# Sharing projection weights between two chunks and staging weight sums in another buffer, in a fused attention and feed-forward kernel

## The chip, the cores and the metric

The kernel runs on one core of one Trainium2 chip. The metric is the device time of one execution in microseconds (us), given as the median of the runs. The kernel before took 834.39 us (median of 3 runs, 833.3 to 835.75).

The engines are named as in the profile: PE (TensorE, matmuls), PEld (its weight loads), DVE (VectorE), ACT (ScalarE), POOL (GpSimd) and SP (SyncE). SP and POOL also issue DMA transfers. In these traces each engine runs its own instructions in a fixed order and stops at the first one that has to wait: in one run below, DVE stood 19.9 us at one operation with others behind it.

## The reference

```python
# x: 2048 x 1024 bf16; 32 heads of 32; window W = 8, dilation 2; feed-forward width 3584
def reference(A_x, A_wqkv, A_wo, B_x, B_w_gate, B_w_up, B_w_down, gate_w):
    x = A_x
    g = sigmoid((x * gate_w).sum(-1, keepdims=True))
    q, k, v = split_heads(x @ A_wqkv)
    # ... each row attends to rows s, s-2, ..., s-14 (those that exist), softmax
    a = o @ A_wo
    h = gelu(x @ B_w_gate) * (x @ B_w_up)
    b = h @ B_w_down
    return g * a + (1 - g) * b
```

## The kernel before

The 2048 rows are cut into four chunks of 512. The feed-forward part works on two chunks at once (a "super") with a seven-product scheme for 2x2 blocks. For that scheme it needs sums and differences ("forms") of x and of the weights. The forms of the down and wo weights are computed once, early, by `prep_down`. That routine loads weight rows, subtracts them on DVE, and stores the forms in DRAM. The parts that the change touches are these; cuts are marked with "...".

```python
ring = ctx.enter_context(tc.tile_pool(name="ring", bufs=5))   # five 1 MB weight tiles
hT = persist.tile([P, 2 * NST, FT, P], BF16)                  # the FFN's hidden values

def qkv_load(which, pieces):          # two ring tiles for q, k or v weights, loaded by SP
    ...
def qkv(c):
    ...
    for which in range(3):
        tiles = qkv_load(which, ...)  # each chunk loads q, k and v weights anew
        ...                           # 64 matmuls, evictions on ACT (and DVE for q of chunk 0)

def x_forms():                        # four DVE operations; the FFN of a super needs all of them
    b11, b21, b12, b22 = xr[:, 0], xr[:, 1], xr[:, 2], xr[:, 3]
    with hp():
        nc.vector.tensor_tensor(out=tf[:, 0], in0=b12, in1=b11, op=ALU.subtract)
        nc.vector.tensor_tensor(out=tf[:, 1], in0=b22, in1=tf[:, 0], op=ALU.subtract)
        nc.vector.tensor_tensor(out=tf[:, 2], in0=b21, in1=tf[:, 1], op=ALU.subtract)
        nc.vector.tensor_tensor(out=b12, in0=b22, in1=b12, op=ALU.subtract)   # "the last x form"

def load_xT(c):                       # eight DMA transposes of x into xr
    for kt in range(KT):
        nc.sync.dma_start_transpose(out=xT(c, kt), in_=x[s0:s0 + SC, kt * P:(kt + 1) * P])

def prep_down(i0, n):                 # called nine times: seven for w_down, two for wo
    ...
        st = ring_tile()              # loaded rows
        ...                           # two loads of 512 KB, issued by POOL
        ot = ring_tile()              # the sums
        fo = ...
        nc.vector.tensor_tensor(out=fo[:, 0], in0=b12, in1=b11, op=ALU.subtract)
        nc.vector.tensor_tensor(out=fo[:, 1], in0=b22, in1=fo[:, 0], op=ALU.subtract)
        nc.vector.tensor_tensor(out=fo[:, 2], in0=b22, in1=b12, op=ALU.subtract)
        nc.vector.tensor_tensor(out=fo[:, 3], in0=b21, in1=fo[:, 1], op=ALU.subtract)
        ...                           # four stores of 256 KB to DRAM, issued by POOL

qkv(0)
...
load_xT(1)
gate(0)
for i0 in range(0, NPREP, 2):
    prep_down(i0, min(2, NPREP - i0))
    if i0 == 6:
        attention(0)                  # DVE work almost alone
qkv(1)
gate(1)
attention(1)
for sup in range(NSUP):
    x_forms()
    ffn(sup)
    ...
```

The program order is not the order on an engine: a scheduler interleaves independent work, and `hp()` raises the priority of what it encloses. `q`, `k` and `v` below are the three parts of the qkv projection.

## Time and profile before

| Reading | Before | View |
|---|---|---|
| median of runs | 834.39 us | times |
| span of the profiled run, granted clock | 833.0 us, 0.950 | page, list of cores |
| PE / DVE busy | 90% / 73% | page, part 1 |
| longest idle stretch of PE | 53.17 us from 56.5 us | timeline of PE |
| SP's longest wait for a ring tile | 71.4 us | waits of SP |
| last x form starts | 158.17 us | timeline of DVE |
| last product of the first FFN ends | 340.09 us | timeline of DVE |

First come lines of the page of the kernel before. Part 1 has busy time, share and instruction count per engine. In part 2 each digit is the busy share, in tenths, of one fortieth of the span (20.8 us); PEclk is the granted clock.

```profile
span 833.0 us, 9110 instructions
PE 746.3 (90%) x3345; PEld 370.1 (44%) x3413; DVE 608.4 (73%) x908; ACT 307.6 (37%) x513; POOL 54.1 (6%) x99
...
PE   7970069899999999799999989979999999999998
...
DVE  1688997999899999771197998998999943641201
...
PEclk8995569999999999899999999989999999999999
DMA  9568884535465465999736895325444444689985
```

The row of PE has two zeros at slices 4 and 5 and nothing like them later. The clock falls to 5 in the same place. DVE and DMA are busy there.

The timeline of PE before has start, length, engine, line, operation, output and inputs, count, and in brackets the idle time before it with what ended it.

```profile
10.73 44.09 PE L137 MATMUL ps<-xr,rg 128*128 128x512 bf16 x188 [3.96 <-DVE xr L518]
54.66 1.89 PE L171 MATMUL pz<-xr,gwb 128*128 128x512 bf16 x8
109.72 3.21 PE L137 MATMUL ps<-xr,rg 128*128 128x512 bf16 x7 [53.17 <-DMA rg<-in_A_wqkv_dram]
```

After the gate of chunk 0 nothing runs for 53.17 us, until a load of qkv weights for chunk 1 lands. The first seven matmuls after the hole take 3.21 us, twice their usual time.

The waits of SP's queue before give total, count and longest in us.

```profile
SPq L129 <- DMA dforms<-rg: 71.4, 1, 71.4
```

This is why the weights were late: the load had to wait for a ring tile that the staging still held until its stores to DRAM ended.

The table of stretches before has start and end, length, busy time (count) of PE, PEld, DVE, ACT and POOL, then granted clock, DMA share and GB/s.

```profile
55.00:110.00 55.00, 1.83 (x9) 0.69 (x7) 48.51 (x110) 3.48 (x5) 23.60 (x41) 0.55 0.84 294
155.00:325.00 170.00, 163.90 (x735) 73.69 (x749) 163.94 (x248) 101.35 (x171) 6.93 (x13) 0.99 0.49 160
```

In the hole DVE is busy 48.5 of 55 us, so DVE limits how much of it can be won. In the FFN, PE and DVE are both full: 163.9 of 170 us.

The FFN can't run on without the last x form. The timeline of DVE before shows when it comes:

```profile
158.17 1.22 DVE L252 TENSOR_TENSOR xr<-xr 128x2048 bf16<-128x2048 bf16 x1
```

### The profile page before, as it was taken

Reading aid. Unit: us, or ns where it says so; the run is one execution under the profiler, and the core shown is the slowest. Engines: PE = TensorE matmul, PEld = TensorE weight load, DVE = VectorE, ACT = ScalarE, POOL = GpSimd, SP = SyncE. Lnnn points to the kernel's source line nnn. Section 1 sums busy time; section 2 is a strip of 40 time slices with the busy share of each in tenths; the row PEclk is TensorE's granted clock in tenths of the full one; section 3 lists DMA queues with packets and bytes.
Section 4 is the critical chain, followed back from the end, with each engine's and each line's share of the span. In section 5 each row is a group of like instructions: output and inputs, shape, how many; then the busy total and the mean of one; then the engine's idle time right before and its main releaser. Section 6 shows DMA issues by size and latency. Waiting matters only on the chain.

```text
span 833.0 us, 9110 instructions
## 1 busy us (share of the span) xinstructions
PE 746.3 (90%) x3345; PEld 370.1 (44%) x3413; DVE 608.4 (73%) x908; ACT 307.6 (37%) x513; POOL 54.1 (6%) x99
## 2 busy tenths in 40 slices
PE   7970069899999999799999989979999999999998
PEld 4640036444444444344664446634444444444443
DVE  1688997999899999771197998998999943641201
ACT  1321014555755457110333104347557555310110
POOL 0044400000000000001000010000000000001000
PEclk8995569999999999899999999989999999999999
DMA  9568884535465465999736895325444444689985
GB/s 307 147 231 296 257 326 134 169 101 159 146 202 157 149 200 164 256 312 331 262 116 220 312 344 171 114 67 173 141 134 168 146 143 160 223 289 312 327 310 185
DMA packets 124491, 174.13 MB, mean 209 GB/s; under 512 B 17696, under 2 KB 96544, under 8 KB 120864
## 3 DMA queue, kind: packets, MB, share of 16 engines
q1 hardware_dynamic: 115488, 136.33, 50.5%
q0 software_dynamic: 8672, 36.71, 12.1%
q8 instruction: 26, 0.43, 0.2%
q10 hardware_dynamic: 288, 0.52, 0.2%
q14 instruction: 17, 0.14, 0.1%
HBM read 142.08 MB, written 28.31 MB: 205 GB/s over the span
## 4 chain that ended last, share of the span: by engine, by line
issue 47%; PE 26%; DVE 17%; DMA 5%; POOL 3%; ACT 2%; POOLq 0%; DVEq 0%; ACTq 0%
PE pB L324 5%; PE qB L447 5%; PE qD L447 4%; PE qA L447 4%; DMA rg<-in_B_w_down_dram 3%; PE pD L324 3%; PE pA L324 3%; DVE prod L202 3%; DVE acc L203 2%; PE ps L137 2%; DVE pall L240 2%; POOL fforms L306 1%; DMA gcol<-in_gate_w_dram 1%; DVE accT L205 1%; DVE hT L350 1%
## 5 line engine op out<-in xcount | busy, mean ns | idle before, releaser
L324 PEld LDWEIGHTS <-rg 128*128 128x128 bf16 x1568 | 154.2, 98 | 203.6 <-issue 22.1
L137 PE MATMUL ps<-xr,rg 128*128 128x512 bf16 x752 | 172.1, 389 | 60.9 <-DMA rg<-in_A_wqkv_dram 56.0
L137 PEld LDWEIGHTS <-rg 128*128 128x128 bf16 x768 | 110.5, 144 | 122.0 <-DMA rg<-in_A_wqkv_dram 58.5
L324 PE MATMUL pB<-tf,rg 128*128 128x512 bf16 x439 | 114.7, 381 | 4.2 <-DVE hT L363 3.6
L324 PE MATMUL pA<-xr,rg 128*128 128x512 bf16 x439 | 114.1, 380 | 2.9 <-ACT pB L344 2.1
L447 PEld LDWEIGHTS <-hT 128*128 128x128 bf16 x672 | 66.3, 99 | 86.2 <-issue 4.7
L447 PE MATMUL qB<-rg,hT 128*128 128x512 bf16 x330 | 76.3, 379 | 0.5 <-DMA rg<-dforms 0.2
L203 DVE TENSOR_TENSOR acc<-acc,prod 128x2048 bf16<-128x2048 bf16 x56 | 68.3, 1220 | 1.2
L324 PE MATMUL pB<-xr,rg 128*128 128x512 bf16 x218 | 57.5, 382 | 5.2 <-DVE og L181 4.7
L324 PE MATMUL pD<-xr,rg 128*128 128x512 bf16 x220 | 56.9, 379 | 2.4 <-ACT m_1678 L358 1.3
L324 PE MATMUL pD<-tf,rg 128*128 128x512 bf16 x220 | 58.7, 388 | 0.2
L447 PE MATMUL qA<-rg,hT 128*128 128x512 bf16 x220 | 54.0, 394 | 4.5 <-DMA rg<-in_B_w_down_dram 4.2
L350 DVE TENSOR_TENSOR hT<-hT,gl 128x1024 bf16<-128x1024 bf16 x56 | 38.3, 685 | 15.5 <-ACT hT L349 15.2
L344 ACT COPY pB<-pA 128x512 f32<-128x512 f32 x56 | 32.2, 576 | 32.8 <-PE pA L324 31.8
L369 ACT ACTIVATE gl<-pA 128x512 bf16<-128x512 f32 x56 | 33.6, 599 | 27.4 <-PE pA L324 25.2
L451 POOL DMA_DIRECT2D out_dram<-ost x24 | 13.0, 541 | 446.9 <-ACT ost L473 339.7
L491 DVE SCALAR_TENSOR_TENSOR ost<-qB,omg,m5d 128x512 bf16<-128x512 f32 x8 | 6.0, 748 | 47.1 <-issue 28.7
L240 DVE TENSOR_TENSOR pall<-ab,vT_85 128x2048 bf16<-128x2048 bf16 x32 | 38.9, 1217 | 0.0
L240 DVE TENSOR_TENSOR pall<-ab,vT_86 128x2048 bf16<-128x2048 bf16 x32 | 38.9, 1216 | 0.0
L505 ACT ACTIVATE ost<-qB,omg 128x512 bf16<-128x512 f32 x8 | 5.5, 687 | 87.6 <-PE qB L447 87.6
L202 DVE TENSOR_TENSOR prod<-qo_81,kT_83 128x2048 bf16<-128x2048 bf16 x28 | 34.2, 1222 | 1.9 <-ACT kT_83 L164 0.5
L349 ACT CAST hT<-pB 128x512 bf16<-128x512 f32 x56 | 32.2, 575 | 7.5 <-PE pB L324 7.5
(649 smaller groups left out, 846.5 us busy)
## 6 DMA issues: line engine op xcount, KB each, us to landing
rg<-dforms SPq DMA_DIRECT2D x32, 896.0 KB, 7.0
rg<-in_A_wqkv_dram SPq DMA_DIRECT2D x22, 1024.0 KB, 8.3
rg<-in_B_w_down_dram SPq DMA_DIRECT2D x24, 896.0 KB, 6.3
rg<-in_B_w_gate_dram SPq DMA_DIRECT2D x28, 512.0 KB, 4.0
fforms<-rg POOLq DMA_DIRECT2D x14, 1024.0 KB, 6.1
rg<-fforms SPq DMA_DIRECT2D x14, 1024.0 KB, 4.8
rg<-oforms SPq DMA_DIRECT2D x16, 512.0 KB, 3.7
rg<-in_B_w_down_dram POOLq DMA_DIRECT2D x14, 512.0 KB, 4.9
```

The lines of the kernel that those rows point to most:

```text
L137: nc.tensor.matmul(ps[:], lhsT=lhsT, rhs=xT(c, kt), start=(kt == 0), stop=(kt == KT - 1))
L202: nc.vector.tensor_tensor(out=prod[:], in0=q_b, in1=k_w, op=ALU.mult)
L203: nc.vector.tensor_tensor(out=acc[:], in0=acc[:], in1=prod[:], op=ALU.add)
L205: nc.vector.transpose(out=accT[:].rearrange("p c d -> p (c d)"), in_=acc[:].rearrange("p w s -> p (w s)"))
L240: nc.vector.tensor_tensor(out=pall[:], in0=ab[:], in1=v_w, op=ALU.mult)
L324: nc.tensor.matmul(bk[:], lhsT=w, rhs=rhs[:, k, :], start=(start and k == 0), stop=(k == KH - 1), skip_group_check=True)
L344: nc.scalar.copy(out=Bk[f][:], in_=A[f][:])
L349: nc.scalar.copy(out=hs(f, 0), in_=v3(Bk[f][:]))
L350: nc.vector.tensor_tensor(out=hT[:, :, f, :], in0=hT[:, :, f, :], in1=gl[f][:].rearrange("p (j s) -> p j s", s=P), op=ALU.mult)
L369: nc.scalar.activation(out=gl[f][:, 0:SC], in_=A[f][:], func=ACT.Gelu_apprx_tanh)
L447: nc.tensor.matmul(bk[:], lhsT=l, rhs=w[i], start=(start and i == 0), stop=(i == n - 1), skip_group_check=True)
L451: eng.dma_start(out=o2[s0 + j * P:s0 + (j + 1) * P, nh * NW:(nh + 1) * NW], in_=ost)
```

## The change

Its intent is to remove the hole. The q, k and v weights are loaded once and kept for both chunks 0 and 1 (6 MB less to load; v weights lie in part of `hT`, which is idle then). The staging of the weight sums moves out of the ring into five stages in `hT`. The gate gets a higher priority. The transposes of chunk 1 move ahead of the q weights in SP's queue, and `attention(0)` moves from after the fourth of the nine stagings to after the last.

```diff
-    def qkv_load(which, pieces):
+    def qkv_load(which, pieces, vbuf=False):
         tiles = []
         for hf in range(2):
-            wt = ring_tile()
-            wv = wt[:].rearrange("p (k n) -> p k n", k=KH)
+            if vbuf:
+                wv = hT[:, hf * KH:(hf + 1) * KH, 0:NT, :].rearrange("p k f n -> p k (f n)")
+            else:
+                wv = ring_tile()[:].rearrange("p (k n) -> p k n", k=KH)
 ...
+    def stage():
+        f0 = 8 + 4 * (stage_n[0] % 5)
+        stage_n[0] += 1
+        return hT[:, :, f0:f0 + 4, :].rearrange("p (a b) f s -> p a b (f s)", b=2)
 ...                                    # in prep_down:
-            st = ring_tile()
+            st = stage()
+            sa, sb = st[:, 0:m, :], st[:, 2:2 + m, :]
+            for dst, r in ((sa, b), (sb, nr + b)):
+ ...
+                for k in range(m):     # four loads of 256 KB a staging, instead of two of 512 KB
+                    nc.gpsimd.dma_start(out=dst[:, k], in_=v[:, k])
-            ot = ring_tile()
+            fo = stage()[:, :, 0:m, :]
 ...
-    qkv(0)
+    load_xT(1)
+    wq = qkv_load(0, [(k, k + 1) for k in range(KH)])
+    qkv_outer(0, 0, wq)
+    wk = qkv_load(1, [(0, KH)])
+    qkv_one(0, 1, wk)
 ...
-    load_xT(1)
-    gate(0)
+    wv = qkv_load(2, [(0, KH)], vbuf=True)
+    qkv_one(0, 2, wv)
+    with hp():
+        gate(0)
     for i0 in range(0, NPREP, 2):
         prep_down(i0, min(2, NPREP - i0))
-        if i0 == 6:
-            attention(0)
-    qkv(1)
-    gate(1)
+    attention(0)
+    halo(1)
+    qkv_one(1, 0, wq)
+    qkv_one(1, 1, wk)
+    qkv_one(1, 2, wv)
+    with hp():
+        gate(1)
     attention(1)
 ...                                    # the other two gates get hp() too
```

More of the change, by code (lines that the diff above doesn't have):

```diff
@@ L137, in qkv_mm, with halo @@
         nc.tensor.matmul(ps[:], lhsT=lhsT, rhs=xT(c, kt), start=(kt == 0), stop=(kt == KT - 1))
-    def qkv(c):
+    def halo(c):
         cc = c % 2
@@ L144, in qkv, with qkv_dst, qkv_outer, qkv_one @@
             nc.scalar.copy(out=vT[cc][:, :, 0:HALO], in_=vT[pc][:, :, SC:SC + HALO])
-        for which in range(3):
-            tiles = qkv_load(which, [(k, k + 1) for k in range(KH)] if (c == 0 and which == 0) else [(0, KH)])
-            dsts = [(qo[cc][:, t, :], kT[cc][:, t, HALO:HALO + SC], vT[cc][:, t, HALO:HALO + SC])[which]
-                    for t in range(NT)]
-            if c == 0 and which == 0:
-                banks = [bank("ps") for t in range(NT)]
-                for kt in range(KT):
-                    for t in range(NT):
-                        qkv_mm(banks[t], tiles, t, kt, c)
-                for t in range(NT):
-                    if t % 2 == 0:
-                        nc.scalar.copy(out=dsts[t], in_=banks[t][:])
-                    else:
-                        nc.vector.tensor_copy(out=dsts[t], in_=banks[t][:])
-            else:
-                for t in range(NT):
-                    ps = bank("ps")
-                    for kt in range(KT):
-                        qkv_mm(ps, tiles, t, kt, c)
-                    nc.scalar.copy(out=dsts[t], in_=ps[:])
+    def qkv_dst(c, which, t):
+        cc = c % 2
+        return (qo[cc][:, t, :], kT[cc][:, t, HALO:HALO + SC], vT[cc][:, t, HALO:HALO + SC])[which]
+    def qkv_outer(c, which, tiles):
+        banks = [bank("ps") for t in range(NT)]
+        for kt in range(KT):
+            for t in range(NT):
+                qkv_mm(banks[t], tiles, t, kt, c)
+        for t in range(NT):
+            if t % 2 == 0:
+                nc.scalar.copy(out=qkv_dst(c, which, t), in_=banks[t][:])
+            else:
+                nc.vector.tensor_copy(out=qkv_dst(c, which, t), in_=banks[t][:])
+    def qkv_one(c, which, tiles):
+        for t in range(NT):
+            ps = bank("ps")
+            for kt in range(KT):
+                qkv_mm(ps, tiles, t, kt, c)
+            nc.scalar.copy(out=qkv_dst(c, which, t), in_=ps[:])
+    def qkv(c):
+        halo(c)
+        for which in range(3):
+            qkv_one(c, which, qkv_load(which, [(0, KH)]))
     gates = {}
@@ L257, in load_xT @@
             nc.sync.dma_start_transpose(out=xT(c, kt), in_=x[s0:s0 + SC, kt * P:(kt + 1) * P])
+    stage_n = [0]
+    def stage():
+        f0 = 8 + 4 * (stage_n[0] % 5)
+        stage_n[0] += 1
+        return hT[:, :, f0:f0 + 4, :].rearrange("p (a b) f s -> p a b (f s)", b=2)
     def prep_down(i0, n):
@@ L264, in prep_down @@
             b, m = (lo[0] if kind == "d" else lo[0] - FH), len(lo)
-            st = ring_tile()
-            sa = st[:, 0:2 * D].rearrange("p (k n) -> p k n", k=2)[:, 0:m, :]
-            sb = st[:, 2 * D:4 * D].rearrange("p (k n) -> p k n", k=2)[:, 0:m, :]
-            if kind == "d":
-                nc.gpsimd.dma_start(out=sa, in_=src[b * P:(b + m) * P, :].rearrange("(k p) n -> p k n", p=P))
-                nc.gpsimd.dma_start(out=sb, in_=src[(FH + b) * P:(FH + b + m) * P, :].rearrange("(k p) n -> p k n", p=P))
-            else:
-                nc.gpsimd.dma_start(out=sa, in_=AP(src.tensor, src.offset + b * D, [[NT * D, P], [D, m], [1, D]]))
-                nc.gpsimd.dma_start(out=sb, in_=AP(src.tensor, src.offset + (NTH + b) * D,
-                                                   [[NT * D, P], [D, m], [1, D]]))
-            ot = ring_tile()
-            fo = ot[:].rearrange("p (f k n) -> p f k n", f=4, k=2)[:, :, 0:m, :]
-            b11, b12, b21, b22 = sa[:, :, 0:NW], sa[:, :, NW:D], sb[:, :, 0:NW], sb[:, :, NW:D]
+            st = stage()
+            sa, sb = st[:, 0:m, :], st[:, 2:2 + m, :]
+            for dst, r in ((sa, b), (sb, nr + b)):
+                if kind == "d":
+                    v = src[r * P:(r + m) * P, :].rearrange("(k p) (h n) -> p k h n", p=P, h=2)
+                else:
+                    v = AP(src.tensor, src.offset + r * D, [[NT * D, P], [D, m], [NW, 2], [1, NW]])
+                for k in range(m):
+                    nc.gpsimd.dma_start(out=dst[:, k], in_=v[:, k])
+            fo = stage()[:, :, 0:m, :]
+            b11, b12, b21, b22 = sa[:, :, 0], sa[:, :, 1], sb[:, :, 0], sb[:, :, 1]
             nc.vector.tensor_tensor(out=fo[:, 0], in0=b12, in1=b11, op=ALU.subtract)
@@ L545 @@
             qkv(c0 + 2)
-            gate(c0 + 2)
+            with hp():
+                gate(c0 + 2)
             attention(c0 + 2)
@@ L551 @@
             qkv(c0 + 3)
-            gate(c0 + 3)
+            with hp():
+                gate(c0 + 3)
             attention(c0 + 3)
```

## The prediction

> **What bounds it now.** The page gives 833.0 us, PE busy 90%. The PE timeline has one large hole: the gate of chunk 0 ends at 56.5 us and the first qkv matmul of chunk 1 starts at 109.72, 53.17 us idle, released by a DMA into `rg` from wqkv. The DMA queue's own waits give the cause: SP's next wqkv load waited 71.4 us for `dforms<-rg`; the sums of down and wo weights hold the five ring slots. The table of stretches shows a granted clock of 0.55 there; the first seven matmuls after the hole take 3.21 us instead of 1.5. The Trainium skill ("TensorE: Matmul & The Clock Gate", Part 1) says that an idle array falls to half rate; this trace agrees (0.50 from 60 to 105 us).
>
> The first FFN is balanced: from 155 to 325 us PE and DVE are each busy 163.9 of 170 us. DVE takes sums, attention and FFN operations in one fixed order and hardly waits from its last x form (L252, 158.2 us) to its last FFN product (about 340): 181 us.
>
> **What changes.** Six wqkv loads (1 MB, 8.3 us each to landing) vanish, and staging no longer holds the ring. Staging makes 36 loads of 256 KB instead of 18 of 512 KB, off the path. PE and DVE work stay the same. The x transposes now stand before the q weights in SP's queue: eight at 1.26 us of issue each, so I estimate that PE starts qkv near 16 us, not 10.7, and ends q near 33, not 27.5.
>
> PE then does both chunks without a hole (44 + 2 + 42 + 2 us) and could start the FFN near 107 instead of 157.5. DVE can't quite follow: by the instruction order, with durations from the trace, it has 88 us of work before the last x form (126 before), of which only 11 stand before the q evictions at 33 us. 33 + 77 = 110 us, plus waits for ScalarE (3 us) and for staging loads, which now compete with k and v weights (the skill's "DMA: Bandwidth & Descriptors", Queues: the engines take turns between queue rows; the trace shows 285 GB/s when staging ran alone). I put the last x form at 118 us (110 to 126), 41 earlier. From there DVE has 183 us of work to the last FFN product (182 before), so the FFN ends near 300 instead of 340. What follows keeps its order; attention of chunk 1 leaves 60 us of DVE work after that point instead of 23, still below the 74 until attention of chunk 2 starts. So of the 53 us hole plus 4 of cold clock, about 41 are gained; the later start and DVE's order take the rest.
>
> **Predicted:** 793 us, 8 in 10 between 782 and 806. Faster by over 2%: 0.94; within 2%: 0.05; slower: 0.01.
>
> **Right or wrong by the profile.** The hole at 56 us is gone; first qkv matmul near 16 us; PE waits 5 to 10 us for DVE at the FFN's start; DVE over 95% busy in the first FFN; from down of chunk 0 on as long as before; clock above 0.97.
>
> **What would make it wrong.** Staging through `hT` slower than thought, DVE stuck behind its loads (805 or more); q, k or v weights late because staging takes half of the DMA engines; or DVE waiting little, the last x form at 108 (783). Attention of chunk 1 ending late could delay chunk 2.

## The result and the profile after

The changed kernel is correct. It took 804.94 us (median of 4 runs, 803.07 to 807.56), against 835.07 us (833.3 to 838.09, 4 runs) for the kernel before on the same chip. Ratios here are the mean time of one kernel's runs over that of the other's of the same rounds, so not quite the ratio of the quoted medians. For the change the ratio is 0.9638, with a 95% interval of 0.9595 to 0.9681. The profiled run has a span of 801.9 us at a granted clock of 0.976.

Lines of the page after, the same parts as before (a slice is now 20.0 us):

```profile
span 801.9 us, 9175 instructions
PE 748.0 (93%) x3413; PEld 369.6 (46%) x3413; DVE 610.5 (76%) x908; ACT 305.3 (38%) x513; POOL 74.3 (9%) x117
...
PE   2679997999999997999999999799998999999998
...
DVE  1467889999999899789979989989999833631201
...
PEclk7789999999999999999999999999999999999999
DMA  9999831354645467988458875325444454779984
```

PE and DVE do the same work as before (748.0 against 746.3 us, 610.5 against 608.4; a few matmul records were missing before). The two zeros are gone. But the first slice of PE has fallen from 7 to 2: a smaller hole has opened at the start.

The timeline of PE after shows it:

```profile
26.81 16.53 PE L139 MATMUL ps<-xr,rg 128*128 128x512 bf16 x68 [19.69 <-DMA rg<-in_A_wqkv_dram]
48.41 15.94 PE L139 MATMUL ps<-xr,rg 128*128 128x512 bf16 x60 [5.07 <-DMA rg<-in_A_wqkv_dram]
...
76.48 1.89 PE L180 MATMUL pz<-xr,gwb 128*128 128x512 bf16 x8
78.21 1.67 PE L139 MATMUL ps<-xr,hT 128*128 128x512 bf16 x7
79.72 27.79 PE L139 MATMUL ps<-xr,rg 128*128 128x512 bf16 x128
...
133.12 0.61 PE L338 MATMUL pB<-xr,rg 128*128 128x512 bf16 x1 [4.88 <-DVE xr L261]
```

PE starts the projection at 26.81 us instead of 10.73, waits another 5.07 us for k weights, and then goes from chunk 0 to chunk 1 (79.72 us) without a stop. At the start of the FFN it waits 4.88 us for the last x form.

In the waits of SP's queue after, no wait for `dforms` is left in the first 135 us. The longest entry is the FFN's first weights waiting for PE to finish with the shared weights; it starves nobody:

```profile
SPq L311 <- PE ps L139: 50.3, 2, 37.6
```

The table of stretches after:

```profile
0.00:15.00 15.00, 5.29 (x37) 3.39 (x37) 2.44 (x8) 3.73 (x6) 6.00 (x13) 0.82 0.88 138
15.00:30.00 15.00, 3.19 (x8) 1.36 (x9) 6.27 (x8) 0.00 (x0) 5.07 (x7) 0.50 1.16 262
30.00:45.00 15.00, 13.34 (x62) 8.46 (x59) 5.68 (x10) 2.05 (x4) 9.41 (x13) 0.99 1.04 393
45.00:60.00 15.00, 11.60 (x41) 6.24 (x42) 10.41 (x12) 2.93 (x5) 9.40 (x13) 0.77 1.05 390
60.00:75.00 15.00, 15.00 (x72) 9.93 (x71) 11.31 (x14) 5.24 (x10) 9.42 (x13) 1.00 0.96 317
75.00:90.00 15.00, 15.00 (x71) 9.64 (x70) 11.57 (x19) 4.53 (x10) 10.06 (x15) 1.00 0.79 245
90.00:119.00 29.00, 29.00 (x137) 19.23 (x135) 24.93 (x68) 11.49 (x19) 5.42 (x9) 1.00 0.56 185
...
150.00:300.00 150.00, 145.54 (x667) 65.08 (x666) 145.88 (x225) 90.93 (x157) 6.38 (x12) 1.00 0.54 174
```

For the first 60 us the DMA engines are nearly full, yet in the first 15 us they move only 138 GB/s. From 30 to 90 us DVE is busy 39.0 of 60 us, although its work is what the FFN will have to wait for. In the FFN both engines are as full as before.

What the DMA engines were doing is in the list of DMA issues after, for the first 22 us (output and input, issuing queue, operation, count, size where it is given, median us from issue to landing). Before, the five transposes that fell into the stretch from 2 to 22 us took a median of 6.1 us to land, and all eight 5.3 us.

```profile
hT<-in_B_w_down_dram POOLq DMA_DIRECT2D x7, 256.0 KB, 13.8
...
xr<-in_A_x_dram SPq DMA_TRANSPOSE x8, 13.7
```

The staging no longer waits for the ring, so its loads start at 2.66 us and run beside the transposes. The q weights stand behind the transposes in SP's queue. The timeline of SP after, from 0 to 45 us, shows how long that queue was held:

```profile
1.66 20.96 SPq L266 DMA_TRANSPOSE xr<-in_A_x_dram  x8
22.67 5.25 SPq L131 DMA_DIRECT2D rg<-in_A_wqkv_dram  x10
```

Issuing the eight transposes took 20.96 us, 2.62 us each, where the prediction counted 1.26. The first q weights were issued only at 22.67 us.

The waits of DVE after, in the first 135 us (total, count, longest):

```profile
DVE hT L292 <- DMA hT<-in_B_w_down_dram: 9.4, 4, 4.6
...
DVE tf L258 <- DMA xr<-in_A_x_dram: 5.7, 1, 5.7
...
DVE hT L294 <- DMA hT<-in_B_w_down_dram: 4.2, 3, 1.6
DVE hT L293 <- DMA hT<-in_B_w_down_dram: 3.8, 3, 1.5
DVE hT L293 <- DMA hT<-in_A_wo_dram: 3.2, 2, 2.2
```

With a fifth entry of 0.4 us, the sums (L292 to L295) wait 21.0 us for staging loads. Before, the corresponding waits were 3.8 us. The last x form, in the timeline of DVE after, is this one:

```profile
131.84 1.22 DVE L261 TENSOR_TENSOR xr<-xr 128x2048 bf16<-128x2048 bf16 x1
```

It comes 26.3 us earlier than before (158.17). The last product of the first FFN ends at 313.01 us instead of 340.09, 27.1 us earlier. The span is 31.1 us shorter. So most of the gain (26.3 of 31.1 us) is the earlier last x form.

### The profile page after: what moved, and what is told of

It reads as the page before. It is cut to its first block, busy times and chain, and to the rows that moved or that the text cites. A ratio compares the mean times of both kernels' runs of the same rounds, so it can differ in the third digit from the quotient of the medians.

```text
span 801.9 us, 9175 instructions
## 1 busy us (share of the span) xinstructions
PE 748.0 (93%) x3413; PEld 369.6 (46%) x3413; DVE 610.5 (76%) x908; ACT 305.3 (38%) x513; POOL 74.3 (9%) x117
## 4 chain that ended last, share of the span: by engine, by line
PE 46%; DVE 34%; DMA 8%; issue 6%; ACT 3%; POOL 2%; SPq 1%; DVEq 0%; ACTq 0%; POOLq 0%
PE pB L338 9%; PE qB L461 8%; PE pD L338 6%; PE qD L461 6%; PE pA L338 6%; DVE pall L249 6%; PE qA L461 5%; PE ps L139 5%; DVE prod L211 3%; DVE acc L212 3%; DMA hT<-in_B_w_down_dram 3%; DMA xr<-in_A_x_dram 2%; DVE hT L377 2%; DVE hT L364 2%; POOL dforms L298 1%
## 5 line engine op out<-in xcount | busy, mean ns | idle before, releaser
L338 PEld LDWEIGHTS <-rg 128*128 128x128 bf16 x1568 | 153.9, 98 | 209.5 <-issue 23.5
L139 PE MATMUL ps<-xr,rg 128*128 128x512 bf16 x640 | 144.2, 388 | 25.5 <-DMA rg<-in_A_wqkv_dram 25.5
L139 PEld LDWEIGHTS <-rg 128*128 128x128 bf16 x640 | 92.0, 144 | 76.8 <-DMA rg<-in_A_wqkv_dram 27.0
L211 DVE TENSOR_TENSOR prod<-qo_81,kT_83 128x2048 bf16<-128x2048 bf16 x28 | 34.2, 1222 | 2.4 <-ACT kT_83 L168 1.3
L211 DVE TENSOR_TENSOR prod<-qo_82,kT_84 128x2048 bf16<-128x2048 bf16 x28 | 34.2, 1221 | 0.8
```

What stands on the lines that cost most here:

```text
L139: nc.tensor.matmul(ps[:], lhsT=lhsT, rhs=xT(c, kt), start=(kt == 0), stop=(kt == KT - 1))
L211: nc.vector.tensor_tensor(out=prod[:], in0=q_b, in1=k_w, op=ALU.mult)
L338: nc.tensor.matmul(bk[:], lhsT=w, rhs=rhs[:, k, :], start=(start and k == 0), stop=(k == KH - 1), skip_group_check=True)
```

## The experiments

The question was why the last x form came only 26.3 us earlier, when the prediction had said 41. One theory said that the late start did it (PE starts at 26.8 us instead of 16, because the transposes stand before the q weights and share the DMA engines with the staging loads). A rival said that DVE's load of work, above all its 36 sums of 0.68 us, did it. A third theory was formed when these two had been tested: the sums stand early in DVE's fixed order, each waits for a chain of load, sum and store through five stages, and this chain is exposed where DVE has nothing else to do first. In the expectations below, "theory A" is the late start, "theory B" and "staging loop" are early forms of the third, "DVE theory" is the rival about DVE's work and order, and "present theory" is the third.

"Last x form" below is its start in the profiled run. "DVE idle" is 93 us less DVE's busy time in the stretch from 26 to 119 us, from the table of stretches. "Staging waits" are DVE's waits for staging loads up to 135 us. Each kernel was run 4 times, and each correct kernel agrees with the reference.

| Kernel | median us | ratio to before (95%) | first qkv matmul | last x form | DVE idle | staging waits |
|---|---|---|---|---|---|---|
| before | 835.07 | | 10.73 | 158.17 | 9.2 | 3.8 |
| the change | 804.94 | 0.9638 (0.9595 to 0.9681) | 26.81 | 131.84 | 25.3 | 21.0 |
| e1_xt_after_q | 808.20 | 0.9683 (0.9657 to 0.9709) | 10.49 | 135.38 | 27.1 | 23.0 |
| e1_xt_last | 807.65 | 0.9675 (0.9650 to 0.9699) | 10.30 | 132.82 | 30.8 | 15.5 |
| e2_hold_stage | 803.31 | 0.9629 (0.9602 to 0.9656) | 15.14 | 126.25 | 27.6 | 18.9 |
| g1_hold_landed | 807.45 | 0.9677 (0.9633 to 0.9722) | 16.07 | 131.60 | 27.7 | 33.0 |
| f1_tiny_sums (wrong result) | 817.95 | 0.9808 (0.9755 to 0.9862) | 23.90 | 136.29 | 41.0 | 38.4 |
| f2_few_loads (wrong result) | 794.74 | 0.9530 (0.9472 to 0.9588) | 22.69 | 119.01 | 12.2 | 5.3 |
| k4_att_at6 | 795.31 | 0.9529 (0.9482 to 0.9576) | 23.22 | 122.10 | 15.8 | 10.2 |
| k6_att_at2 | 798.49 | 0.9578 (0.9515 to 0.9641) | 22.16 | 120.11 | 15.2 | 4.9 |
| k5_att_at2_hold | 797.62 | 0.9555 (0.9497 to 0.9613) | 15.17 | 119.01 | 18.4 | 11.1 |
| e4_stage_only | 818.40 | 0.9797 (0.9753 to 0.9841) | 27.71 | 144.22 | 37.1 | 31.2 |
| e3_gate_plain | 807.26 | 0.9677 (0.9652 to 0.9701) | 28.14 | 132.88 | 26.2 | 18.0 |
| h1_pool_sums | 850.68 | 1.0184 (1.0124 to 1.0244) | 25.69 | 176.57 | 16.5 | 0 |

The diffs are against the changed kernel. The kernels ran in four groups, each beside runs of the kernel before on the same chip. Its medians were 834.96 us (e1, e2, e3), 831.92 (f1, f2, g1, h1), 834.2 (e4, k4, k5) and 834.63 (k6).

### Is it the late start? The transposes moved behind the q weights

```diff
-    load_xT(1)
     wq = qkv_load(0, [(k, k + 1) for k in range(KH)])
+    load_xT(1)          # e1_xt_after_q; in e1_xt_last it stands after the v weights
     qkv_outer(0, 0, wq)
```

> Change with one edit: the eight x transposes of chunk 1 stand behind the q weights in SP's queue, as before the change, instead of ahead of them. Theory A (the late start, 26.8 us instead of 10.7, is paid in full down to the last x form): first qkv matmul at 11 to 12 us, end of q near 30, last x form near 118 instead of 131.8, time about 790 us. Theory B (the loop of staging loads, sums and stores sets when DVE reaches the last x form, wherever PE starts): first qkv matmul early as well, but last x form at 128 or later and the time within 4 us of the change.

> The transposes behind all six qkv weight loads (q, k, v). Theory A: first qkv matmul at 11 to 12 us and no wait for k weights, so at least as good as behind q alone, 785 to 790 us, unless DVE, whose order puts the x forms ahead of some q evictions, waits for the late transposes (they would land near 40 us) and holds the PSUM banks of k: then PE shows a wait of about 10 us after q. Theory B: within 4 us of the change.

Both kernels start the projection at 10.3 to 10.5 us, 16 us earlier than the change. Neither is faster than the change: 808.20 and 807.65 us. So starting PE earlier in this way wins nothing, and theory A missed. In e1_xt_after_q the eight transposes still take 20.87 us to issue, now ahead of the k weights, for which PE waits 7.78 us. The waits of DVE in e1_xt_last show where those 16 us went:

```profile
DVE tf L258 <- DMA xr<-in_A_x_dram: 19.9, 1, 19.9
```

DVE has an x form (L258) early in its order, and now stands there 19.9 us for the transposes. The wait for DMA has moved from PE to DVE.

### The transposes free of staging: hold the staging until q is done

Three one-column copies into the first stages make the staging loads wait for the projection of q.

```diff
     qkv_outer(0, 0, wq)
+    for f0 in (8, 16, 24):
+        nc.scalar.copy(out=hT[:, :, f0, 0:1], in_=qo[0][:, :, 0:1])
```

> The change, but staging held until q is evicted (three small copies on ScalarE write into the first stages, so the loads wait for them); transposes still first in the queue. It tells whether the transposes are late of themselves or because staging loads share the DMA engines. If contention makes them late: each lands in 5 to 6 us as before instead of 13.7, first qkv matmul near 16 us (what the prediction assumed). If not: they still land late and qkv starts after 24. The total: staging starts some 20 us later, so under theory B the last x form is later than 131.8 and the kernel slower than the change; under theory A about 10 us faster.

In the list of DMA issues of e2_hold_stage for the first 22 us, the transposes land in less than a quarter of the time:

```profile
xr<-in_A_x_dram SPq DMA_TRANSPOSE x8, 3.1
```

Their issue is short again too, in the timeline of SP from 0 to 45 us:

```profile
1.66 10.32 SPq L266 DMA_TRANSPOSE xr<-in_A_x_dram  x8
```

So running beside the staging loads is the cause of the late transposes, and PE starts at 15.14 us, as the prediction had it. The last x form comes only 5.6 us earlier: from the end of q (32.5 us) it took 93.8 us, against 88.1 in the change. The time, 803.31 us, can't be told from the change's, so both theories missed on it. The staging waits are still 18.9 us: the loads that were held now come later.

g1_hold_landed releases the staging earlier, when the last q weights have landed (the copies stand before the projection and read the last piece of `wq`).

```diff
     wq = qkv_load(0, [(k, k + 1) for k in range(KH)])
+    for f0 in (8, 16, 24):
+        nc.scalar.copy(out=hT[:, :, f0, 0:1],
+                       in_=wq[1][:, KH - 1, 0:8].rearrange("p (a o) -> p a o", o=1))
     qkv_outer(0, 0, wq)
```

> As the held staging (803.3 us), but held only until the last q weights have landed, some 10 us earlier. First qkv matmul at 15 us as there; staging starts near 18 us and shares the engines with k and v weights. DVE theory: DVE has the sums to do while it would wait for q (13.9 us idle there), so the last x form comes some 5 us earlier than with the longer hold, at 119 to 123, time 794 to 799 us.

This missed what was expected. PE starts at 16.07 us, but the sums wait 33.0 us for staging loads, one of them for 13.5 us, and PE waits 9.1 us for DVE to evict q, which stands behind those sums. The time is 807.45 us. Neither hold of the staging loads, nor either placement of the transposes, brought a gain in time as long as all the sums stood ahead of attention in the program.

### Is it DVE's work? The sums cut to 16 of 512 columns

This gives a wrong result. Two memsets fill the stages that would be stored without having been written.

```diff
-            nc.vector.tensor_tensor(out=fo[:, 0], in0=b12, in1=b11, op=ALU.subtract)
+            nc.vector.tensor_tensor(out=fo[:, 0, :, 0:16], in0=b12[:, :, 0:16], in1=b11[:, :, 0:16], op=ALU.subtract)
 ...                                    # the other three likewise
+    for f0 in (12, 20):
+        nc.vector.memset(hT[:, :, f0:f0 + 4, :], 0.0)
     load_xT(1)
```

> Wrong on purpose: each of the 36 sums on DVE covers 16 columns instead of 512, so that loads, stores, their order and what waits for what stay, and some 19 us of DVE work go. If DVE's work in its fixed order sets the time (the theory after the first runs: last x form plus some 672 us is the time), the last x form comes as early as PE lets it, at 122 to 124 us, attention of chunk 2 starts 15 to 19 us earlier than in the change (385), and the time is 784 to 790 us. Rival: the loop of staging loads and stores through the DMA engines sets it; then DVE only waits longer at the same sums, the last x form stays at 129 or later and the time within 4 us of the change.

DVE is busy 15.7 us less between 26 and 119 us (52.0 against 67.7), so it idles that much more. The time went up, to 817.95 us. The waits of DVE in f1_tiny_sums:

```profile
DVE hT L292 <- DMA hT<-in_B_w_down_dram: 14.6, 5, 3.7
DVE hT L293 <- DMA hT<-in_B_w_down_dram: 12.6, 4, 7.8
```

This speaks against the theory that the amount of DVE work sets the time: DVE waits for the staging loads instead of summing. It is not a clean test. The rival had expected a time within 4 us of the change, and it came out 13 us slower, which isn't settled; the scheduler also placed the instructions in another order.

### Is it the staging loads? Two thirds of them left out

This also gives a wrong result: only the first three of the nine stagings load anything. Sums and stores stay.

```diff
-                for k in range(m):
+                for k in range(m if i0 < 6 else 0):
                     nc.gpsimd.dma_start(out=dst[:, k], in_=v[:, k])
```

> Wrong on purpose: only the first three of the nine stagings load their rows, the others sum what the stages hold; 6 MB less to move, sums and stores all there. Under the DVE theory only DVE's waits for those loads go, 12 us after 45 us by the list of DVE's waits: last x form at 119 to 123, time 790 to 796 us. If the DMA traffic of the stretch is the deeper cause, more is gained than these waits, since k weights and transposes land earlier as well: last x form at 115 or earlier (PE permitting) and no wait for k weights. If neither counts: unchanged.

The staging waits fall from 21.0 to 5.3 us, DVE's idle time by 13.1 us, and the last x form comes 12.8 us earlier. The time is 794.74 us. The time and the last x form both lie in the ranges expected if only DVE's waits for these loads go. What was expected of the DMA traffic as the deeper cause (115 us or earlier, no wait for k weights) did not come: PE still waits 3.75 us for k weights. From the end of DVE's last q eviction (40.1 us) to the last x form are 78.9 us, against 88.1 in the change. All sums are still made, so it was the wait for the loads, not the work of the sums, that held DVE up.

### The other way to cover the loads: attention back among the stagings

If the third theory holds, the loads needn't be faster; DVE needs something else to do while they are on their way. In the kernel before, attention of chunk 0 stood after the fourth staging. k4_att_at6 undoes just this part of the change.

```diff
         prep_down(i0, min(2, NPREP - i0))
-    attention(0)
+        if i0 == 6:                    # k4_att_at6; i0 == 2 in k6_att_at2
+            attention(0)
```

> One part of the change undone: attention of chunk 0 stands again after the fourth of the nine stagings, not after all of them, so DVE's order has fewer sums ahead of attention and spreads them out. Present theory: DVE waits less for staging loads (21 us in the change): 8 to 14 us, last x form at 122 to 127, time 795 to 801 us. Rival (the engines' bytes alone set when the sums are done, not the order): last x form at 129 to 133, within 4 us of the change.

This kernel is correct and takes 795.31 us (793.11 to 799.44); time, last x form and waits all lie in the ranges expected of the present theory. It beats both kernels; its interval (0.9482 to 0.9576) lies below the change's (0.9595 to 0.9681). Its stretches, to set beside those of the change:

```profile
45.00:60.00 15.00, 15.00 (x63) 9.01 (x63) 10.94 (x13) 4.40 (x8) 8.68 (x12) 0.89 1.05 383
60.00:75.00 15.00, 15.00 (x71) 9.62 (x70) 15.00 (x18) 4.68 (x9) 13.15 (x19) 1.00 1.02 352
75.00:90.00 15.00, 15.00 (x71) 9.97 (x70) 14.68 (x59) 5.50 (x11) 9.32 (x13) 1.00 0.71 244
90.00:119.00 29.00, 29.00 (x136) 18.70 (x135) 28.41 (x43) 11.55 (x18) 1.13 (x2) 1.00 0.50 161
```

From 60 to 119 us DVE (the third busy time) is now busy 58.1 of 59 us, against 47.8 for the change. The DMA share is as high as before: the loads take as long, but DVE does attention meanwhile. DVE idles 9.5 us less from 26 to 119 us, and the last x form comes 9.7 us earlier. The first projection also starts earlier here (23.22 us), and DVE's last eviction of q ends at 41.2 us instead of 43.7. That may account for up to 2.5 us. The other 7.2 us come after it: from there to the last x form are 80.9 us instead of 88.1. The timeline of DVE in k4_att_at6:

```profile
122.10 1.22 DVE L261 TENSOR_TENSOR xr<-xr 128x2048 bf16<-128x2048 bf16 x1
```

One link of the chain was left untested. POOL issues the loads and the stores of the sums in one order, and a store waits for its sum. The timeline of POOL in the change shows six loads that were issued only when the sums before them were done:

```profile
53.87 0.73 POOL L298 DMA_DIRECT2D dforms<-hT  x1 [0.29 <-DVE hT L295]
54.59 4.33 POOL L289 DMA_DIRECT2D hT<-in_B_w_down_dram  x6
```

In the first 100 us POOL stood 39.7 us at stores that waited for sums, with later loads behind them. Issuing took it 0.73 us a transfer, 52.2 us for the staging's 72; in the kernel before, up to 110 us, 53 transfers took 31.5 us. The loads issued between 60 and 75 us took a median of 4.8 us to land, no longer than the 4.9 us of the 512 KB loads before. So a part of DVE's waits may come from late issue and not from busy DMA engines. f2_few_loads removes both at once, and no kernel issued the loads from another queue.

k6_att_at2 puts attention after the second staging, and k5_att_at2_hold adds the hold of e2_hold_stage to that.

> The order effect carried further, without the hold: attention of chunk 0 after the second of the nine stagings. Present theory: DVE's waits for staging loads after q go down from about 10 us (attention after the fourth) to under 6, last x form at 116 to 121, but PE ends chunk 1 at 118 to 119 and must be done with x first, so at most 4 us are left: 788 to 796 us. Rival (the gain of the earlier placing was the scheduler's luck): 800 us or more.

> Attempt at a faster kernel: attention of chunk 0 after the second staging, and staging held until q is evicted, so that transposes and qkv weights have the engines first. Present theory: first qkv matmul at 15 us as with the hold alone; the sums stand later in DVE's order than there, so the waits for staging loads (19 us there) mostly go: last x form at 114 to 121 instead of 126, time 788 to 796 us. Rival: the waits move with the sums, 799 to 804 us as with the hold alone.

In k6_att_at2 the staging waits fall further, to 4.9 us, and the last x form comes at 120.11 us, another 2.0 us earlier. But the time is 798.49 us, not better, and above the expected 788 to 796. From the last x form to the last FFN product it took 183.8 us, against 179.9 in k4_att_at6, so the gain was given back inside the FFN. k5_att_at2_hold starts at 15.17 us, has its last x form in the expected range (119.01 us), and takes 797.62 us, just above the expected 796. The intervals of k4, k5 and k6 overlap, so no order among the three is shown.

### What the parts of the change are worth: staging alone

Chunk 1 loads its own q, k and v weights again, and the v weights go back into the ring. What is left is the staging in `hT` and the new order.

```diff
-    wv = qkv_load(2, [(0, KH)], vbuf=True)
+    wv = qkv_load(2, [(0, KH)])
 ...
-    halo(1)
-    qkv_one(1, 0, wq)
-    qkv_one(1, 1, wk)
-    qkv_one(1, 2, wv)
+    qkv(1)
```

> One half of the change alone: sums staged in the h buffer, but chunk 1 loads its own qkv weights (6 MB more through the ring, as before the change). Present theory (after the tiny sums and the few loads: in the first 95 us DVE waits, in its fixed order, for staging loads whose trip is long because the DMA engines are full): 6 MB more at some 390 GB/s are 15 us of full engines, so the last x form comes at 138 to 147 us instead of 132 and the time is 811 to 820 us. Rival: freeing the ring is what matters and sharing is an extra: within 4 us of the change. Either way the 53 us hole of the kernel before is gone.

It takes 818.40 us, as expected: about 16 us less than the kernel before beside it (834.2; the interval of the ratio, 0.9753 to 0.9841, lies below 1), and 13.5 us more than the change. So moving the staging out of the ring, with what else is left of the diff, is about half of the gain. The shared loads are the other half: without them, 6 MB more pass through the DMA engines (at the 390 GB/s that the trace of the change shows from 30 to 60 us I estimate 16 us), the staging waits rise to 31.2 us and the last x form comes 12.4 us later than in the change.

### The gate's priority

```diff
-    with hp():
-        gate(0)
+    gate(0)
 ...                                    # and so for all four gates
```

> The change without the raised priority of the gate. Both theories: within 1% of the change, since the gate of chunk 1 can't release its PSUM bank before attention of chunk 0 has left the shared tile; at most a PE wait of 5 us comes or goes at the FFN's start.

It takes 807.26 us; the interval overlaps the change's, so a gain of the priority isn't shown. The waits of PE in e3_gate_plain, from 298 us on, do show a wait that the kernel before had too (4.7 us) and that the change has not:

```profile
PE pB L338 <- DVE og L190: 5.4, 1, 5.4
```

Here PE waits for DVE, which is at the gate's arithmetic. With the priority this wait is gone, but PE then waits 4.1 us for ACT's copy of `m` in the same part of the program. The wait moved more than it vanished.

### The sums on GpSimd

```diff
-            nc.vector.tensor_tensor(out=fo[:, 0], in0=b12, in1=b11, op=ALU.subtract)
+            nc.gpsimd.tensor_tensor(out=fo[:, 0], in0=b12, in1=b11, op=ALU.subtract)
 ...                                    # the other three likewise
```

> Correct kernel: the 36 sums on GpSimd instead of DVE. DVE theory: as with the tiny sums, last x form at 122 to 126 and 785 to 792 us, unless GpSimd is so slow that staging ends after 150 us and holds the h stages (then a wait for dforms stores in the FFN), or slows DVE by sharing. Rival (staging loop): a slower loop on GpSimd makes it worse than the change.

This takes the sums and their waits out of DVE's order altogether. The time is 850.68 us, 1.2 to 2.4% slower than the kernel before. The groups of instructions of h1_pool_sums from 40 to 140 us (busy time and mean ns of one; then idle time before):

```profile
L211 DVE TENSOR_TENSOR prod<-qo,kT 128x2048 bf16<-128x2048 bf16 x7 | 22.1, 3159 | 0.6
...
L293 POOL TENSOR_TENSOR hT<-hT 128x1024 bf16<-128x1024 bf16 x7 | 16.0, 2280 | 6.5 <-DMA hT<-in_B_w_down_dram 6.2 <-DMA hT<-in_A_wo_dram 0.2
```

A sum takes 2280 to 2461 ns on GpSimd, against 677 to 690 ns on DVE in the change. Worse, DVE's own products take 3159 ns instead of 1222 while GpSimd sums. The Trainium skill ("GPSIMD Engine Reference", 1. Specifications) says that GpSimd's SBUF interfaces are shared with VectorE, with contention for DVE instructions that have two SBUF inputs. This run agrees: these products have two, and are 2.6 times as long. The page's 3.1 gives about 2.6 cycles per element for such an operation; at its 1.2 GHz I estimate 2219 ns for 1024 elements, a little under the 2280 to 2461 measured beside DVE's work.

## Why the prediction was right or wrong

The direction and the main mechanism were right: the hole went, and DVE kept part of it. The time of 804.94 us lies inside the range of 782 to 806, but only by 1.1 us, and the middle, 793, was 11.9 us too low. The last x form, on which the sum turned, came outside its own range (131.84 us; 110 to 126 predicted). The time stayed inside because its range was wide and because what follows was some 3 us shorter than forecast (671.8 us in the profiled run of 803.67, against 793 less 118). That part is luck.

| Step | Predicted | Measured |
|---|---|---|
| hole at 56 us | gone | gone |
| first qkv matmul | near 16 us | 26.81 us |
| q ends (DVE's last eviction of it) | near 33 us | 43.7 us |
| from the end of q to the last x form | 85 us (77, and 8 of waits) | 88.1 us |
| last x form | 118 us | 131.84 us |
| last x form to last FFN product | 183 us | 181.2 us |
| first FFN ends | near 300 us | 313.0 us |
| the rest of the program | 493 us (793 less 300) | 490.7 us (803.67 of the profiled run, less 313.0) |
| PE's wait for DVE at the FFN's start | 5 to 10 us | 4.9 us |
| DVE in the first FFN | over 95% | 145.88 of 150 us, 97% |
| granted clock | above 0.97 | 0.976 |

**The cause of the old time was right.** The staging held the ring, PE idled 53 us and its clock fell. The Trainium skill ("TensorE: Matmul & The Clock Gate", Part 1), which the prediction cites, has an idle array at half rate; the trace before shows 0.50 from 60 to 105 us. The new, smaller hole shows the same: 0.50 from 15 to 30 us.

**That DVE would keep part of the hole was right.** In all correct kernels except h1_pool_sums the FFN's last product ends 179 to 184 us after the start of the last x form. The part after the last FFN product is 489 to 495 us in every one of these traces. So the time is the last x form and a nearly fixed remainder; the change won 26.3 of its 31.1 us of span before that point. The other 4.8 us are within what the remainder varies, and I give them no cause.

**The terms that were mis-sized are the start of q and the waits for staging loads.** The prediction put "that PE starts qkv near 16 us", from "eight at 1.26 us of issue each", with about 5 us for the sums' waits "for staging loads". Both took their times from a trace in which the staging did not yet run so early. With the loads freed at 2.66 us, the eight transposes took 20.96 us to issue instead of about 10, and 13.7 us to land instead of 5.3. The sums waited 21.0 us for loads, 13.0 of them after the end of q. The Trainium skill ("DMA: Bandwidth & Descriptors", Queues, rings and completion order) says that the engines take turns between queue rows packet by packet. The prediction cited it for k and v weights and didn't apply it to the transposes, where e2_hold_stage shows a large effect of the shared traffic (3.1 us against 13.7). That the packets alternate is not itself visible in these runs; that the two streams slow each other is.

**But the late start isn't the whole cause, and repairing it isn't the remedy.** By its place in the sum, the late end of q explains 10.7 of the 13.8 us by which the last x form was late. But e2_hold_stage, which ends q earlier than the predicted 33 us, gets back only 5.6, and the two e1 runs start before 10.5 us and win nothing. In each run somebody waits for data: PE for q weights, or DVE for transposes, or DVE for staging loads. How much of this comes from full DMA engines (a DMA share of 0.88 to 1.16 in the first 60 us of the change) and how much from late issue by POOL isn't separated. What k4_att_at6 shows is that it matters whether DVE has other work while it waits. f2_few_loads (less to load) and k4_att_at6 (attention among the stagings) both reach 795 us, and in both the last x form moves by as much as DVE's idle time shrinks (12.8 and 13.1 us; 9.7 and 9.5 us). The other runs don't all follow this count: in k5_att_at2_hold the last x form is 12.8 us earlier with 6.9 us less idle time in the same stretch. The move of `attention(0)` behind all stagings, a side effect of the diff that the prediction did not cost by itself, is worth about 9 us (the ratios of the two kernels to the kernel before differ by 0.0109, of 834 us).

**What was named as a way to be wrong came true.** "DVE stuck behind its loads (805 or more)" describes the measured kernel.

**Left open:** how much of DVE's waits is due to POOL's order of stores and loads; why f1_tiny_sums is slower than the change rather than equal to it; why the FFN of k6_att_at2 takes 4 us longer than that of k4_att_at6; and why the first projection starts at 22 to 28 us in kernels whose code before that point is the same.

## What to carry to other kernels

When a change frees a buffer, the transfers that used to wait for it start earlier and compete with whatever is then on the critical path; take their new landing times from a trace with the same traffic, not from the old one. If the engine that feeds the next stage runs in a fixed order, put independent work between operations that wait for DMA: this won about 9 us here, where moving or holding the transfers by itself won nothing that could be measured. A hole on PE is worth only what the second engine lets through, so cost that engine's work up to the next point where the two meet.

## What the Trainium skill lacked or had wrong

- "DMA: Bandwidth & Descriptors", Latency and other measured facts, gives an effective bandwidth for DMA transposes but not what they suffer or cause beside other traffic. Here eight transposes took a median of 13.7 us to land beside seven staging loads of 256 KB, and 3.1 us without them; with both, the first 15 us moved 138 GB/s at a DMA share of 0.88, against 393 GB/s at 1.04 between 30 and 45 us.
- "DMA: Bandwidth & Descriptors", Specifications, has about 358 GB/s as the HBM limit of a core, with no condition in that row but the division by two cores. This program on one core moved 393 and 390 GB/s over two stretches of 15 us in the change. The page's own Bandwidth section ties the lower figure to both cores of a pair streaming, which no run here shows; the row should say so.
- "GPSIMD Engine Reference", 4.1 Engine selection, has two-input operations about twice as slow on GpSimd as on VectorE; the page's measurement in 3.1 is in fp32. In bf16 with 128x1024 elements, and with DVE at work beside it, the ratio was 3.3 to 3.6 (2280 to 2461 ns against 677 to 690).
